# When pieces of the output weights are cast and stored, where the gate is computed, and which queue makes the first loads

## The chip, the cores and the metric

The kernel runs on one core of one Trainium2 chip. The time is the device time of one launch in microseconds (us). Three runs of the kernel before took 2896.23, 2896.97 and 2898.16 us; the median is 2896.97 us. The profiled execution took 2899.53 us, and its span from the first to the last instruction is 2897.4 us.

## The reference

One input `x` of 2048 tokens by 1024 features goes through two attention blocks of 32 heads (32 features each). A gate per token mixes their results. All in fp32.

```
qkv = x @ wqkv                          # for A and for B, each with its own weights
A: phi(t) = where(t > 0, t + 1, exp(t)) + 1e-6
   kv = phi(k)^T v ; z = sum(phi(k)) ; o = phi(q) kv / (phi(q) z + 1e-6)
   a = o @ A_wo
B: p = softmax(q k^T / sqrt(32)) ; o = p v
   b = o @ B_wo
g = sigmoid(sum(x * gate_w, -1))
out = g * a + (1 - g) * b
```

## The kernel before

**Matmuls.** A large product is made from a high and a low fp32r part of each side: three matmuls of 128x128 by 128x512 on TensorE (PE), high by high, low by high and high by low (the function `three`, L153 to L158). The split into parts is a ScalarE (ACT) cast for the high part and a subtraction on VectorE (DVE) or GpSimd (POOL) for the low part (`split`, L294 and L295).

**Stages.** (1) Until about 435 us the projections of block B, in two halves of 1024 tokens: a pass for 512 columns of v, and eight `quad`s, each a 2x2 block product by a Strassen-like scheme of seven products (X11, X21, X22, T1 to T4). The parts of x that these products read lie in pairs of the large buffers `big0` to `big13`, by the table `PLACES`. (2) From about 435 to 520 us the "v" chunk: the other columns of v, and the first row maxima of block B's scores for head 0. (3) From about 520 to 2720 us 32 heads of block B run beside the linear work of block A, which goes through the kinds "kv" (to about 1740 us), "q" (to about 2130 us) and "o". (4) At the end the output product of block B, again as a 2x2 scheme of seven products (`output`).

**A head.** For each 128x512 tile of scores PE makes it once for the row maximum (L1170; DVE reduces it out of the PSUM bank, L1175) and once for the exponential (L1312; ACT writes it to SBUF, L1315). PE then multiplies the exponentials by v (L1462, in groups of eight key tiles, some 7 us each). POOL adds up the exponentials of the key tiles (L1393, L1397), on 1536 or 512 columns at a time; DVE adds the last 512 columns in a PSUM bank (L1413), inverts the sum (L1244) and scales the result (L1247). Six or seven PSUM banks are shared by maxima, exponentials and linear work (`take`, `give`).

**What sets the order.** The kernel writes every engine's instructions in a fixed order that its own planner makes while the program is built. It keeps an assumed clock for each engine (`T`), appends work to an engine with an assumed cost (`use`), and holds back DVE work in a list `later` with a due time, cost and rank (`defer`); `fill` appends such an item when the assumed DVE clock leaves room. The chip then runs the fixed order; only semaphores decide the times. Transfers that are written with `dma` all go in order through SyncE's queue (SP, L170): a transfer that waits for its buffer holds up those behind it. `dma_start` on `nc.gpsimd` uses POOL's queue.

**Weights of the output product.** Its right sides are W11, W12, W22 and four sums S1 to S4 of blocks of `b_wo`. `wo_sums` makes the sums on POOL in the two halves of the buffer `zrep` (L501 to L523), by way of loads and stores on POOL's queue. In order of the program it stands beside the first half's quads, but POOL has nothing before it that waits for them. Later, during "o", `pre_split` takes 28 pieces (seven right sides, four pieces each) of 128x512: it loads a piece through SP, casts it on ACT (L1508) when the assumed clock is 4.5 us past the load, subtracts on DVE (L1511, deferred), and appends the two stores to SP together with the subtraction. `load_w_op` loads the finished right sides back, in the order of `w_next`.

**The gate.** `gate` loads `gate_w` to all partitions, and in the "v" chunk 16 tiles of x (128x1024) through SP into the halves of `big12`; DVE multiplies each by `gate_w` and sums along the row (L534).

**First loads of the heads.** For heads 0 and 1 the stacked parts of q and k (`load_q`, `load_k`: 36 transfers) go through SP in the "v" chunk, from the list `first`.

**Share of the linear work.** `rates` says how many linear matmuls go with each step of the heads; `RESERVE` (56.0) is the part that is held for after the heads.

Of the kernel before, what the change touches and what calls it, by code (L numbers as in the profile page):

```python
# [10 lines left out]
F32 = mybir.dt.float32  # L11
# [8 lines left out]
P = 128  # L20
# [9 lines left out]
RESERVE = 56.0  # L30
# [8 lines left out]
WARM = 8  # L39
NE = 3  # L40
# [8 lines left out]
def kernel(  # L49
# [258 lines left out]
    PLACE = [(6, 7), (8, 9), (10, 11), (12, 13), (0, 1), (2, 3), (4, 5)]  # L308
# [182 lines left out]
    def wo_piece(m, i):  # L491

        if m[0] == "S":
            return so_d[m][i]
        half, l = int(m[1]) - 1, int(m[2]) - 1
        return b_wo[(2 * i + l) * P:(2 * i + l + 1) * P, half * C:(half + 1) * C]

    def wo_sums():

        z0, z1 = halves(zrep)  # L500
        load = lambda z, m, i: nc.gpsimd.dma_start(z, wo_piece(m, i))  # L501
        for _ in range(NP):
            yield
        for i in range(KH):
            load(z0, "W21", i)
            load(z1, "W22", i)
            yield
            nc.gpsimd.tensor_add(z1, z0, z1)
            load(z0, "W11", i)
            nc.gpsimd.dma_start(so_d["S1"][i], z1)  # L510
            yield
            nc.gpsimd.tensor_sub(z1, z1, z0)
            load(z0, "W12", i)
            nc.gpsimd.dma_start(so_d["S2"][i], z1)
            yield
            nc.gpsimd.tensor_sub(z0, z0, z1)
            load(z1, "W21", i)
            nc.gpsimd.dma_start(so_d["S4"][i], z0)
            yield
            load(z0, "W11", i)  # L520
            yield
            nc.gpsimd.tensor_sub(z0, z0, z1)
            nc.gpsimd.dma_start(so_d["S3"][i], z0)  # L523
            yield

    def gate():
        xn = halves_of(big_tile(12, F32))
        junk = halves_of(big_tile(13, F32))[0]
        dma(zrep, bass.AP(tensor=gate_w.tensor, offset=gate_w.offset, ap=[[0, P], [1, D]]))
        for t in range(NT):  # L530
            dma(xn[t % 2], x[t * P:(t + 1) * P, :])
            yield
            use("dve", 1.2)
            nc.vector.scalar_tensor_tensor(junk, xn[t % 2], 1.0, zrep, op0=ALU.mult, op1=ALU.mult,  # L534
                                           accum_out=g_sb[:, t:t + 1])
        nc.scalar.activation(g_sb, g_sb, AF.Exp, scale=-1.0)
        nc.vector.tensor_scalar_add(g_sb, g_sb, 1.0)
        nc.vector.reciprocal(g_sb, g_sb)
        nc.vector.tensor_scalar(omg_sb, g_sb, -1.0, 1.0, op0=ALU.mult, op1=ALU.add)
# [123 lines left out]
    quads(0, lambda: load_pair(raw_x1[0], 1, 0), spill_rest(0), wo_sums())  # L663
# [46 lines left out]
    quads(1, lambda: load_v1(raw_a, range(KH)), spill_rest(1))  # L710
    load_v1(raw_b, range(KH, NK))

    def leave():

        split_v1(raw_a[2], 2)
        split_v1(raw_a[3], 3)
        yield
        xh_t[2] = sb.tile([P, 2 * HK * P], F32R, name="xh")
        split_v1(raw_a[0], 0)
        split_v1(raw_a[1], 1)  # L720
        yield
        for k in range(KH, NK):
            split_v1(raw_b[k - KH], k)
            yield


# [234 lines left out]
    quad(1, QUADS - 1, leave())  # L961
    T["sp"] = 0.0
    for m in range(3):
        xp_ready[m] = 0.0

    def linear():
        extra = iter(())
        gates = gate()
        first = deque()
        for h in range(2):  # L970
            first.append(lambda h=h: load_q(h, 0))
            first.append(lambda h=h: load_k(h, 0))
            first.append(lambda h=h: load_q(h, 1, NJ))
            first.extend(lambda h=h, j=j: load_k(h, j) for j in range(1, NJ))
            first.append(lambda h=h: load_v(h))
        for n, (i, t) in enumerate(units):
# [18 lines left out]
            for k in range(NK):  # L995
# [11 lines left out]
                if kind == "v":  # L1007
                    if first and (k == 1 or k == 5 and n < TPC):
                        first.popleft()()
                    if t > 1 and (k == 3 or k == 7 and t % 2):  # L1010
                        next(gates, None)
# [54 lines left out]
            elif kind == "q":  # L1066
                yield from keys_alone(n - 3)
# [53 lines left out]
    def load_q(h, j, j1=0):  # L1121

        g, r = divmod(h, 4)
        j1 = max(j + 1, j1)
        q, sl = q_cols(h, j, j1), slice(j * C, j1 * C)
        if h < (2 if j else 3):
            nc.gpsimd.memset(f32(q[3 * DH:, :]), 0.0)  # L1127
        else:
            dma(f32(q[3 * DH:3 * DH + 2, :]), f32(q[3 * DH + 2:3 * DH + 4, :]))
        for b, p in enumerate((0, 0, 1)):  # L1130
            dma(f32(q[b * DH:(b + 1) * DH, :]), qk_d[0][p][g][r * DH:(r + 1) * DH, sl])
        for i in range(j, j1):
            q_ready[h][i] = max(T["pe"] + 8.0, T["sp"] + 5.0)

    def load_k(h, j):

        g, r = divmod(h, 4)
        k = k_stack[h % 2]
        if h < 2 and j == 0:
            nc.gpsimd.memset(f32(k[3 * DH:, :]), 0.0)  # L1140
            nc.gpsimd.memset(f32(k[3 * DH:3 * DH + 2, :]), 1.0)
        sl = slice(j * C, (j + 1) * C)
        for b, p in enumerate((0, 1, 0)):
            dma(f32(k[b * DH:(b + 1) * DH, sl]), qk_d[1][p][g][r * DH:(r + 1) * DH, sl])
        k_ready[h][j] = max(T["pe"] + 6.0, T["sp"] + 4.0)
# [344 lines left out]
    coming_p, pair_at, piece_at = deque(), [0.0, 0.0], [0.0]  # L1490
    piece_t = [(mid[0], mid[1]), (mid[6], mid[9])]

    def pre_split():

        if lin_kind[0] != "o" or not (pieces or coming_p):
            return
        n = 4 * len(OPS) - len(pieces)
        if pieces and piece_at[0] <= T["pe"] and pair_at[n % 2] is not None and pair_at[n % 2] <= T["pe"] and s_done[0] > st_done[0]:
            m, i = pieces.popleft()
            dma(piece_t[n % 2][0], wo_piece(m, i))  # L1500
            coming_p.append((m, i, n % 2, T["pe"] + 4.5))
            pair_at[n % 2] = None
            piece_at[0] = T["pe"] + PIECE_STEP
        if coming_p and coming_p[0][3] <= T["pe"]:
            m, i, place, _ = coming_p.popleft()
            raw, hi = piece_t[place]
            at = use("act", 0.63, T["pe"])
            nc.scalar.copy(f32r(hi), raw)  # L1508

            def low(end):  # L1510
                nc.vector.tensor_sub(f32r(raw), raw, hi)  # L1511
                for p, src in enumerate((hi, raw)):
                    dma(wo_d[m][p][:, i * C:(i + 1) * C], src)
                pair_at[place] = end + 4.0

            defer(low, at, 0.9, 2)
# [25 lines left out]
    w_next = ["W11", "S1", "W12", "S3", "W22", "S2", "S4"]  # L1542

    def load_w_op():

        if st_done[0] < (H - 1) * NT * NJ or pieces or coming_p:
            return
# [209 lines left out]

    streams = {"lin": linear(), "max": maxima(), "head": heads_(), "out": output()}
# [43 lines left out]
    while streams or tasks:  # L1802
# [3 lines left out]
        pump_w()  # L1806
        fold_now()
# [70 lines left out]
```

## Time and profile before

| | |
|---|---|
| median of three runs | 2896.97 us |
| profiled execution | 2899.53 us |
| its span | 2897.4 us |
| PE busy | 2827.8 us, 98% |
| DVE busy | 2366.6 us, 82% |
| ACT busy | 1622.7 us, 56% |
| POOL busy | 1961.9 us, 68% |
| mean granted TensorE clock | 0.99 |

How to read the rows shown below. A row of the stretches gives the start and end of a stretch, its length, then for each of PE, PEld (weight load), DVE, ACT and POOL the busy time and the number of instructions, then the mean clock that TensorE was granted (1.00 is full speed), the busy share of the DMA engines and GB/s. In a row of the waits stand the waiting engine with what its instruction writes and its line, then who ended the wait, the total in us, how many waits, the longest. A row of the timeline has start, duration, engine, line, operation, output<-input, how many equal instructions in a row, and in brackets the idle time of the engine before it and what ended that. Groups by line end with busy us, mean ns of one | idle time before them and who ended it. "SPq" is SyncE's queue; its duration there is the time until the transfer was handed over.

### The profile page before, as it was taken

The numbers are of one execution on the slowest core, as the hardware profiler recorded it, in microseconds if no ns is written. First come the engines' busy times: TensorE is split into PE (matmuls) and PEld (weight loads), VectorE is DVE, ScalarE is ACT, GpSimd is POOL, SyncE is SP. The second block draws the span as 40 slices with busy tenths as digits, with TensorE's granted clock in tenths as the row PEclk, the third lists the DMA queues.
The fourth block names the chain that finished last, engine by engine and source line by source line (L and its number), as shares of the span: only waits on it lengthen the run. The fifth ranks groups of instructions, "written<-read, shape, count | busy, mean of one in ns | idle before, by whom it ended". The sixth has DMA issues, their size and how long they took to land.

```text
span 2897.4 us, 46873 instructions
## 1 busy us (share of the span) xinstructions
PE 2827.8 (98%) x15848; PEld 2045.3 (71%) x15848; DVE 2366.6 (82%) x3805; ACT 1622.7 (56%) x3060; POOL 1961.9 (68%) x950
## 2 busy tenths in 40 slices
PE   9999998999999999999999999999988999899999
PEld 7888887767776776677677777777755666566687
DVE  7877748888888888888888888788878888898578
ACT  4334320666676666666666666666655555566422
POOL 3200010699999999998999998899887778777000
PEclk9999999999999999999999999999999999999999
DMA  9977769434433344343433344466666565655675
GB/s 322 304 241 226 221 191 299 135 107 99 120 106 100 93 110 120 96 104 106 117 99 99 102 137 144 148 197 193 178 194 177 167 177 162 182 144 177 235 223 156
DMA packets 410411, 471.57 MB, mean 163 GB/s; under 512 B 107214, under 2 KB 235470, under 8 KB 408380
## 3 DMA queue, kind: packets, MB, share of 16 engines
q1 hardware_dynamic: 393372, 444.98, 50.0%
q0 software_dynamic: 16800, 23.60, 4.4%
q8 instruction: 126, 2.06, 0.3%
q14 instruction: 113, 0.93, 0.1%
HBM read 322.17 MB, written 131.86 MB: 157 GB/s over the span
## 4 chain that ended last, share of the span: by engine, by line
PE 86%; DVE 6%; DMA 5%; issue 1%; SPq 1%; ACT 1%; ACTq 0%; DVEq 0%
PE bank L1312 15%; PE bank L1170 15%; PE bank L1462 14%; PE bank L158 13%; PE bank L153 13%; PE bank L156 13%; DVE mx L1175 2%; DVE mid L1511 1%; SPq L170 1%; DVE big L295 1%; DMA ra<-mid 1%; DMA mid<-soS 1%; DVE bank L1244 1%; DMA big<-oA 1%; DMA v<-mid 1%
## 5 line engine op out<-in xcount | busy, mean ns | idle before, releaser
L1397 POOL TENSOR_TENSOR big<-big,big 128x512 f32<-128x512 f32 (+2 forms) x694 | 1651.0, 2383 | 156.3 <-ACT big L1315 115.0
L1175 DVE TENSOR_REDUCE mx<-bank 128x1 f32<-128x512 f32 x2048 | 1303.9, 682 | 250.3 <-PE bank L1170 246.0
L1315 ACT ACTIVATE big<-bank 128x512 f32<-128x512 f32 x2048 | 1175.1, 602 | 460.5 <-PE bank L1312 399.9
L1312 PE MATMUL bank<-big,big 128*128 128x512 f32 x1888 | 749.8, 398 | 26.8 <-ACT big L1315 12.1
L1170 PE MATMUL bank<-big,big 128*128 128x512 f32 x1888 | 745.4, 395 | 13.6 <-ACT big L1315 9.2
L153 PE MATMUL bank<-big,big 128*128 128x512 f32 x1576 | 619.5, 393 | 9.1 <-ACT big L294 4.4
L156 PE MATMUL bank<-big,big 128*128 128x512 f32 x1576 | 617.8, 392 | 2.7 <-DVE big L295 2.7
L158 PE MATMUL bank<-big,big 128*128 128x512 f32 x1572 | 616.8, 392 | 0.7 <-DMA big<-oA 0.7
L1312 PEld LDWEIGHTS bank<-big,big 128*128 128x128 f32 x1888 | 356.9, 189 | 160.6 <-issue 47.1
L1462 PE MATMUL bank<-big,mid 128*32 128x512 f32 x4096 | 455.6, 595 | 0.0
L1170 PEld LDWEIGHTS bank<-big,big 128*128 128x128 f32 x1888 | 357.2, 189 | 95.1 <-ACT big L1315 13.7
L153 PEld LDWEIGHTS bank<-big,big 128*128 128x128 f32 x1576 | 298.0, 189 | 76.5 <-ACT big L294 6.7
L156 PEld LDWEIGHTS bank<-big,big 128*128 128x128 f32 x1576 | 298.0, 189 | 65.4 <-DVE big L295 3.5
L158 PEld LDWEIGHTS bank<-big,big 128*128 128x128 f32 x1572 | 297.2, 189 | 65.7 <-DVE big L295 1.5
L1462 PEld LDWEIGHTS bank<-big,mid 128*32 128x32 f32 x4096 | 142.5, 110 | 265.9 <-issue 265.9
L1413 DVE TENSOR_TENSOR bank<-bank,big 128x512 f32<-128x512 f32 x364 | 251.2, 690 | 10.8 <-ACT big L1315 9.3
L1127 POOL MEMSET big<- 32x512 f32 (+1 forms) x4 | 3.8, 952 | 230.5 <-PE bank L158 230.5
L1393 POOL TENSOR_TENSOR big<-big,big 128x1536 f32<-128x1536 f32 (+1 forms) x31 | 121.8, 3929 | 55.2 <-ACT big L1315 51.9
L153 PE MATMUL bank<-big,xh 128*128 128x512 f32 x376 | 149.2, 397 | 8.6 <-DMA xh<-xs 7.4
L294 ACT CAST big<-mid 128x512 fp32r<-128x512 f32 (+1 forms) x157 | 92.3, 616 | 116.0 <-DVE mid L1610 66.9
L295 DVE TENSOR_TENSOR big<-mid,big 128x512 fp32r<-128x512 f32 (+1 forms) x157 | 107.0, 696 | 61.1 <-ACT big L294 58.0
L156 PE MATMUL bank<-big,xh 128*128 128x512 f32 x376 | 148.2, 394 | 0.2 <-DMA big<-wa 0.2
(150 smaller groups left out, 2173.9 us busy)
## 6 DMA issues: line engine op xcount, KB each, us to landing
big<-xs SPq DMA_DIRECT2D x288, 256.0 KB
big<-qk SPq DMA_DIRECT2D x720, 64.0 KB
xh<-xs SPq DMA_DIRECT2D x144, 256.0 KB
qk<-mid SPq DMA_DIRECT2D x128, 256.0 KB
big<-oA SPq DMA_DIRECT2D x84, 256.0 KB
xs<-big SPq DMA_DIRECT2D x64, 256.0 KB
oA<-mid SPq DMA_DIRECT2D x64, 256.0 KB
big<-big POOLq DMA_DIRECT2D x50, 256.0 KB, 5.6
```

The costliest lines, as they stand in the source:

```text
L153: yield nc.tensor.matmul(ps, sh, mh_, start=(kt == 0), stop=False)
L156: yield nc.tensor.matmul(ps, sh, ml_, start=False, stop=(late and last))
L158: yield nc.tensor.matmul(ps, sl, mh_, start=False, stop=last)
L295: eng.tensor_sub(lo, src, f32(hi))
L1170: nc.tensor.matmul(bank[b], q[:, t % TPC * P:(t % TPC + 1) * P], k[:, j * C:(j + 1) * C], start=True, stop=True)
L1175: nc.vector.tensor_reduce(m[:, t, j:j + 1], bank[b], AX.X, ALU.max)
L1312: nc.tensor.matmul(bank[b], k[:, t * P:(t + 1) * P], q_cols(h, j), start=True, stop=True)
L1315: nc.scalar.activation(pr_t[i][:, j * C:(j + 1) * C], bank[b], AF.Exp, scale=SCALE)
L1393: nc.gpsimd.tensor_add(lacc[:, :qp], pr(0)[:, :qp], pr(1)[:, :qp])
L1397: nc.gpsimd.tensor_add(lacc[:, sl], lacc[:, sl], pr(t)[:, sl])
L1413: nc.vector.tensor_add(lacc[:, qp:] if t == NT - 1 else l_b[:, :n], l_b[:, :n], src)
L1462: nc.tensor.matmul(av_b[j * DH:(j + 1) * DH, :], v[:, t, :], pr(t)[:, j * C:(j + 1) * C], start=(t == 0), stop=(t == NT - 1))
```

## The change

- `pre_split`: a piece is cast when the assumed clock is 10 us past its load (was 4.5). Its two stores are kept in a list `coming_s` and appended to SP's queue at a later turn, at the earliest 2 us after the assumed end of the subtraction; the buffer pair counts as free 6 us after that end (was 4).
- `wo_sums` is cut into 24 steps. Each begins with a 128x1 copy on ACT and one on POOL that reads it, and takes four turns of the quads' side work; it runs over both halves of the projections.
- The gate leaves the "v" chunk. `gate_step`, called once in each turn of the planner, runs it during "kv": 32 half tiles of 128x512, each loaded through SP to `mid10`, multiplied and summed by one deferred DVE instruction (assumed cost 0.9), with `gate_w` in `mid8` and `mid9`.
- The 36 first loads of q and k for heads 0 and 1 go through POOL's queue (`load_first`), in the last quad.
- `PLACE` changes which buffers some products' sides have; `RESERVE` is 24.0 (was 56.0); `w_next` loads S4 and S2 before W22.

The number of matmuls is the same. ACT has 24 small copies more, POOL 24 small copies and 36 transfers more, DVE 32 instructions of 512 columns in place of 16 of 1024 and one small sum; SP has 36 transfers of q and k less, 16 of x with 1024 columns less and 32 with 512 columns more.

On SP at the start of the "v" chunk (`in_x` is x for the gate, `qk...` the q and k parts, `v1` a result, `xs` the parts of x for the next units, which PE needs). Before:

```order
L170 DMA big12_3282<-in_x 128x1024
L170 DMA big2_208<-qk0_0_0_128 32x512 x2
L170 DMA big2_208<-qk0_1_0_136 32x512
L170 DMA big12_3282<-in_x 128x1024
L170 DMA v1_161<-mid10_234 128x512
L170 DMA big3_209<-qk1_0_0_144 32x512
L170 DMA big3_209<-qk1_1_0_152 32x512
L170 DMA big3_209<-qk1_0_0_144 32x512
L170 DMA big12_3282<-in_x 128x1024
L170 DMA xh_3102<-xs0_13_76 128x512
L170 DMA xh_3102<-xs1_13_92 128x512
```

The same place after:

```order
L171 DMA big4_210<-xs1_13_92 128x512
L171 DMA v1_161<-mid10_234 128x512
L171 DMA v1_161<-mid11_235 128x512
L171 DMA v1_161<-mid10_234 128x512
L171 DMA mid2_226<-v0_160 128x16x32
L171 DMA xh_3284<-xs0_13_76 128x512
L171 DMA xh_3284<-xs1_13_92 128x512
```

The loads for the gate and for q and k no longer stand ahead of the loads of `xs`.

On SP in the "o" stretch, around the first piece of S1 (`soS1_0` is the piece, `woS1_0` and `woS1_1` its stored parts, `oA` the input of the linear units, `wa` other stores). Before:

```order
L170 DMA mid0_224<-soS1_0_260 128x512
L170 DMA oB_127<-mid11_235 32x4x128 x4
L170 DMA wa1_0_1_167<-mid8_232 32x512 x4
L170 DMA wa0_0_1_163<-big12_3952 32x512 x2
L170 DMA woS1_0_278<-mid1_225 128x512
L170 DMA woS1_1_279<-mid0_224 128x512
L170 DMA wa0_0_1_163<-big12_3952 32x512 x2
L170 DMA xh_3102<-oA0_4_99 128x512
L170 DMA xh_3102<-oA1_4_115 128x512
```

After:

```order
L171 DMA mid0_224<-soS1_0_260 128x512
L171 DMA woW11_0_276<-mid9_233 128x512
L171 DMA woW11_1_277<-mid6_230 128x512
L171 DMA xh_3284<-oA0_4_99 128x512
L171 DMA xh_3284<-oA1_4_115 128x512
L171 DMA big1_207<-qk1_0_6_150 32x512
L171 DMA big1_207<-qk1_1_6_158 32x512
L171 DMA big1_207<-qk1_0_6_150 32x512
L171 DMA mid6_230<-soS1_1_261 128x512
L171 DMA woS1_0_278<-mid1_225 128x512
L171 DMA woS1_1_279<-mid0_224 128x512
```

The stores of a piece now stand behind the load of the next piece and behind loads for the linear units.

On DVE in "kv", around the 159th row maximum (`mx` is the maximum, `bank7` the sum of the last 512 columns). Before:

```order
L1175 TENSOR_REDUCE mx0_199<-bank6_244 128x1
L1413 TENSOR_TENSOR bank7_245<-bank7_245,big7_3941 128x512
L1175 TENSOR_REDUCE mx0_199<-bank1_239 128x1
L1175 TENSOR_REDUCE mx0_199<-bank4_242 128x1
L1175 TENSOR_REDUCE mx0_199<-bank3_241 128x1
L1175 TENSOR_REDUCE mx0_199<-bank0_238 128x1
```

After:

```order
L1193 TENSOR_REDUCE mx0_199<-bank1_239 128x1
L1193 TENSOR_REDUCE mx0_199<-bank5_243 128x1
L553 SCALAR_TENSOR_TENSOR mid10_234,g_sb_197<-mid10_234,mid8_232 128x512
L1193 TENSOR_REDUCE mx0_199<-bank3_241 128x1
L1193 TENSOR_REDUCE mx0_199<-bank4_242 128x1
L1193 TENSOR_REDUCE mx0_199<-bank0_238 128x1
```

A gate instruction with two inputs in SBUF (`mid10`, `mid8`) now stands in a run of maxima. There are 32 of these in "kv": 11 of them next to the inverse, the scaling or the other work that lies around a group of products with v, and 21 within a run of maxima.

The diff, cut to its core:

```diff
-RESERVE = 56.0
+RESERVE = 24.0
+GATE_STEP = 12.0
-    PLACE = [(6, 7), (8, 9), (10, 11), (12, 13), (0, 1), (2, 3), (4, 5)]
+    PLACE = [(6, 7), (8, 9), (10, 11), (0, 1), (2, 3), (12, 13), (4, 5)]
...
     def wo_sums():
         z0, z1 = halves(zrep)
+        tokens = count()
+        def step(*fns):
+            n = next(tokens) % (C // DH)
+            nc.scalar.copy(dn[0][:, n:n + 1], eps)
+            nc.gpsimd.tensor_copy(dn[1][:, n:n + 1], dn[0][:, n:n + 1])
+            for fn in fns:
+                fn()
+            for _ in range(4):
+                yield
...
+            yield from step(load(z0, "W21", i), load(z1, "W22", i))
+            yield from step(add(z1, z0, z1), load(z0, "W11", i), store("S1", z1, i))
...
-    def gate():
...
+    gate_w_t = [mid[8], mid[9]]
+    def gate_step():
+        n = gate_n[0]
+        if lin_kind[0] != "kv" or gate_at[0] is None or gate_at[0] > T["pe"] or n > 2 * NT:
+            return
...
+        t, i = divmod(n, 2)
+        xn, to = mid[10], (g_sb, omg_sb)[i]
+        dma(xn, x[t * P:(t + 1) * P, i * C:(i + 1) * C])
+        gate_at[0] = None
+        def part(end):
+            nc.vector.scalar_tensor_tensor(xn, xn, 1.0, gate_w_t[i], op0=ALU.mult, op1=ALU.mult,
+                                           accum_out=to[:, t:t + 1])
+            gate_at[0] = end + GATE_STEP
+        defer(part, T["pe"] + 9.0, 0.9, 2)
...
-    quads(0, lambda: load_pair(raw_x1[0], 1, 0), spill_rest(0), wo_sums())
+    quads(0, lambda: load_pair(raw_x1[0], 1, 0), spill_rest(0), sums_w)
-    quads(1, lambda: load_v1(raw_a, range(KH)), spill_rest(1))
+    quads(1, lambda: load_v1(raw_a, range(KH)), spill_rest(1), sums_w)
+    for _ in sums_w:
+        pass
...
         for k in range(KH, NK):
             split_v1(raw_b[k - KH], k)
+            if 0 < k - KH < 3:
+                load_first(k - KH - 1, 0)
             yield
+        load_first(0, 1)
+        load_first(1, 1)
+    def load_first(h, part):
+        if not part:
+            load_q(h, 0, now=nc.gpsimd)
+            load_k(h, 0, nc.gpsimd)
+        else:
+            load_q(h, 1, NJ, nc.gpsimd)
+            for j in range(1, NJ):
+                load_k(h, j, nc.gpsimd)
...
     def pre_split():
...
+        while coming_s and coming_s[0][0] <= T["pe"]:
+            _, m, i, parts = coming_s.popleft()
+            for p, src in enumerate(parts):
+                dma(wo_d[m][p][:, i * C:(i + 1) * C], src)
...
-            coming_p.append((m, i, n % 2, T["pe"] + 4.5))
+            coming_p.append((m, i, n % 2, T["pe"] + 10.0))
...
                 nc.vector.tensor_sub(f32r(raw), raw, hi)
-                for p, src in enumerate((hi, raw)):
-                    dma(wo_d[m][p][:, i * C:(i + 1) * C], src)
-                pair_at[place] = end + 4.0
+                coming_s.append((end + 2.0, m, i, (hi, raw)))
+                pair_at[place] = end + 6.0
...
-    w_next = ["W11", "S1", "W12", "S3", "W22", "S2", "S4"]
+    w_next = ["W11", "S1", "W12", "S3", "S4", "S2", "W22"]
```

100 lines of the change are left out of this document (40 added, 60 removed).

## The prediction

> **What bounds the kernel.** I read the page first, then the stretches of the span by stage, then who PE waited for in the stretches with idle time, then single waits in the timeline.
>
> ```profile
> span 2897.4 us, 46873 instructions
> PE 2827.8 (98%) x15848; PEld 2045.3 (71%) x15848; DVE 2366.6 (82%) x3805; ACT 1622.7 (56%) x3060; POOL 1961.9 (68%) x950
> ```
>
> ```profile
> 0.00:76.00 76.00, 70.46 (x291) 56.18 (x292) 54.24 (x82) 35.84 (x64) 21.84 (x31) 0.98 0.97 318
> 76.00:430.00 354.00, 354.00 (x1563) 293.10 (x1562) 249.39 (x386) 130.60 (x230) 35.60 (x39) 1.00 0.75 237
> 430.00:550.00 120.00, 109.32 (x467) 87.81 (x465) 92.88 (x157) 31.53 (x59) 16.95 (x7) 0.97 0.79 251
> 550.00:1740.00 1190.00, 1189.73 (x7661) 832.71 (x7663) 1034.61 (x1751) 793.05 (x1535) 1116.81 (x558) 1.00 0.39 106
> 1740.00:2130.00 390.00, 390.00 (x2166) 279.89 (x2159) 320.06 (x521) 247.95 (x478) 345.56 (x133) 1.00 0.56 173
> 2130.00:2660.00 530.00, 488.26 (x2637) 324.84 (x2639) 450.14 (x658) 307.31 (x554) 417.87 (x183) 0.96 0.58 166
> 2660.00:2770.00 110.00, 102.70 (x543) 69.04 (x533) 61.70 (x97) 45.72 (x89) 7.23 (x3) 0.97 0.78 265
> 2770.00:2893.00 123.00, 123.00 (x544) 101.75 (x543) 102.75 (x156) 30.71 (x54) 0.00 (x0) 1.00 0.58 177
> ```
>
> PE is the bound. The matmuls stay the same, so the time can change only by PE's idle time and by its clock. The stretches give both: idle time is length less PE busy; work lost to the clock is length times (1 - clock). That makes 5.5 + 1.5 us in the first 76 us, 10.7 + 3.6 around the "v" chunk, 0.3 in "kv", nothing in "q", 41.7 + 21.2 in "o", 7.3 + 3.3 at the change to the output product: 95 us that a change of order alone could reach. "kv" has nothing to win, only to lose.
>
> **Term 1, sums on POOL.**
>
> ```profile
> 1.33 0.73 POOL L501 DMA_DIRECT2D zrep<-in_b_wo  x1 [0.38 <-issue]
> PE bank L156 <- DVE big L295: 2.7, 1, 2.7
> PE bank L153 <- ACT mid L359: 1.7, 1, 1.7
> ACT mid L359 <- DMA v<-mid: 5.4, 3, 4.6
> L508 POOL TENSOR_TENSOR zrep<-zrep 128x512 f32<-128x512 f32 x4 | 5.3, 1314 | 23.1 <-DMA zrep<-in_b_wo 23.1
> ```
>
> POOL starts its loads at 1.33 us, beside the first loads of x and weights, with the DMA engines at 0.97. ACT then waits 5.4 us for stores of v, and PE 2.7 and 1.7 us; with the clock (1.5) that is 5.9 us. With the sums paced by the quads this traffic is gone until the first quad. I take 4.5 us of gain, between 0 and 5.9, nearer to all of it since both waits come before or with the first quad. The sums come back where PE waits for nothing (76 to 430 us, DMA 0.75, DVE 70% busy): 16 additions of 1.31 us can hold DVE up by 21 us in all, against its 105 us of idle time there, and 24 small copies on ACT stand against 223 idle us. Costed at nothing; if that cover failed, at most some 5 us.
>
> **Term 2, the "v" chunk.**
>
> ```profile
> 427.10 4.51 SPq L170 DMA_DIRECT2D big<-in_x  x1
> 435.52 1.22 DVE L534 SCALAR_TENSOR_TENSOR big<-big,zrep 128x1024 f32<-128x1024 f32 x1 [3.39 <-DMA big<-in_x]
> 436.78 0.36 SPq L170 DMA_DIRECT2D big<-in_x  x1
> 437.25 0.84 SPq L170 DMA_DIRECT2D xh<-xs  x2
> PE bank L153 <- DMA xh<-xs: 7.4, 1, 7.4
> 434.00:450.00 16.00, 8.56 (x29) 6.51 (x28) 3.80 (x7) 0.59 (x1) 0.00 (x0) 0.79 0.99 301
> ```
>
> The load of x for the gate at 436.78 could go only when DVE had done with the buffer (435.52 + 1.22), and the load that PE needs stood behind it. PE lost 7.4 us, and 16 x 0.21 = 3.4 us to the clock afterwards: 10.8. The new order of SP has no gate and no q or k loads ahead of it. I take 10; the bounds are 0 and the stretch's whole 14.3. What is late next is the same load by its own 5 to 6 us of landing, which the planner issues three units ahead. The 36 first loads cost POOL, at the 0.73 us of the row in term 1, 26 us of issue; it is 16.95 us busy from 430 to 550. They go out in the last quad, and head 0 needs the last of them only in the course of the chunk. Price 0, at most the 3 us by which the chunk's other waits could grow.
>
> **Term 3, the pieces in "o".**
>
> ```profile
> PE bank L1312 <- ACT big L1315: 12.9, 3, 8.0
> PE bank L1170 <- ACT big L1315: 9.0, 4, 5.1
> PE bank L1312 <- DVE mx L1175: 7.1, 5, 2.2
> PE bank L1312 <- DVE mid L1247: 7.0, 5, 2.3
> PE bank L1170 <- DVE mx L1175: 4.3, 3, 1.8
> ACT mid L1508 <- DMA mid<-soS: 14.9, 4, 6.0
> ACT mid L1508 <- DMA xh<-oA: 9.0, 1, 9.0
> SPq L170 <- DVE mid L1511: 35.5, 17, 4.8
> 2130.00:2150.00 20.00, 11.81 (x41) 8.53 (x40) 9.92 (x17) 7.54 (x16) 16.27 (x9) 0.74 0.58 194
> 2239.00:2251.00 12.00, 7.96 (x25) 6.01 (x24) 5.99 (x10) 4.99 (x9) 6.20 (x3) 0.72 0.80 222
> 2461.00:2473.00 12.00, 6.93 (x23) 5.14 (x22) 5.42 (x8) 4.76 (x9) 6.33 (x2) 0.72 1.04 247
> ```
>
> PE's waits have two causes. ACT stands at the cast of a piece that has not landed (L1508), the exponentials queue behind it, and PE waits for them: 12.9 + 9.0 = 21.9 us. Three of them also lower the clock: 20 x 0.26 + 12 x 0.28 + 12 x 0.28 = 12.0 us. Together 33.9. The cast now comes 5.5 us later by the assumed clock, which covers most of a single wait (6.0 and 9.0 at the longest), and SP no longer stands 35.5 us for the subtractions, so that the loads go out earlier. But the assumed clock does not know how late SP is, and the first piece still goes out behind the stores and loads at the change to "o". I take two thirds, 22, between 0 and 33.9. The DVE waits (7.1 + 7.0 + 4.3 = 18.4) stay: the subtraction itself is the same.
>
> **Term 4, the gate in "kv".**
>
> ```profile
> L1511 DVE TENSOR_TENSOR mid<-mid,mid 128x512 fp32r<-128x512 f32 x28 | 63.3, 2265 | 9.9 <-ACT mid L1508 9.9
> L295 DVE TENSOR_TENSOR mid<-mid,mid 128x512 fp32r<-128x512 f32 x64 | 44.5, 695 | 37.5 <-ACT mid L294 35.5
> 2502.90 10.95 POOL L1397 TENSOR_TENSOR big<-big,big 128x1536 f32<-128x1536 f32 x3
> 2506.55 3.97 DVE L1511 TENSOR_TENSOR mid<-mid,mid 128x512 fp32r<-128x512 f32 x1
> 2511.17 0.50 PE L1312 MATMUL bank<-big,big 128*128 128x512 f32 x1 [2.18 <-DVE mx L1175]
> DVE mx L1175 <- PE bank L1170: 139.2, 58, 5.7
> ```
>
> The same subtraction of 512 columns takes 0.695 us on average in the projections and 2.265 in "o". The timeline shows why: three POOL additions of 10.95 / 3 = 3.65 us run back to back; the second begins as the subtraction does, and the subtraction ends 0.4 us after it (2510.52 against 2510.20). It waited for POOL; the maxima behind it came late, and PE stood 2.18 us. Its inputs are both in SBUF, while the maxima and the sums of L1413 have one in PSUM. So the 18.4 us of DVE waits, and the clock that "o" lost beyond term 3 (21.2 - 12.0 = 9.2), belong to 28 subtractions: 27.6 / 28 = 0.99 us each.
>
> The gate instruction also has two inputs in SBUF. In the "v" chunk POOL was nearly idle (16.95 of 120 us); in "kv" it is busy 1116.81 of 1190 us, more than in "o" (417.87 of 530), and DVE 1034.61 of 1190. At 0.99 us each, 32 gate steps cost 32 us. Eleven of them stand beside a group of products with v, where DVE's longest idle times lie (58 waits of up to 5.7 us), and may be swallowed; POOL's higher share speaks for more at the other 21. I take 0.8 us each: 26 us of loss. The lower bound is 0: 32 x 0.7 us fit many times into the 139 us. The upper bound puts the whole wait on PE: 32 x (2.265 - 0.695) = 50 us. The 34 loads of the gate have 1190 us on SP and go far ahead of their use: 0.
>
> The Trainium skill ("SBUF — State Buffer", section "Who interferes with whom") says that a DVE instruction with two SBUF inputs contends with a GpSimd instruction that reads SBUF, and that the one that issues second is blocked until the first is done. The trace agrees for the subtraction (3.97 us against 0.695); no row shows it for the gate's multiply with a sum. By that rule the change's sum is the one below; without it the gate would be free and the sum the first rival's.
>
> **Term 5, the end.**
>
> ```profile
> PE bank L153 <- ACT big L294: 4.4, 2, 3.2
> PE bank L153 <- DMA big<-oA: 2.2, 1, 2.2
> ```
>
> The smaller reserve moves 32 matmuls of linear work ahead of the heads' end; at 354 us / 1563 matmuls (76 to 430 us) = 0.23 us each, 7.4 us. Fewer linear units then run back to back on loads of x that land late (2.2 us), but there is less to put beside the last head's sums. I take a gain of 2, between a gain of 6 and a loss of 7.4. The order of `w_next` frees no wait that a row shows: 0.
>
> **Sum.** -4.5 - 10 - 22 + 26 - 2 = -12.5 us against the profiled execution's 2899.53, so 2887.0. The median of the runs lies 2.6 below the profiled one: 2884.5, forecast 2885.
>
> **Rivals.** (a) The gate is hidden, by DVE's idle time or because its instruction does not wait for POOL: term 4 is 0, the sum -38.5, the time 2858. For it: eleven steps in places with idle time, and 139 us of DVE's idle time in the stretch. Against it: 0.99 us per subtraction in "o".
> (b) Slower: the gate's wait behind POOL lies wholly on PE, as DVE in "kv" has no slack in a run of maxima. At 1.20 us a step it eats the other 38.5 us, from 1.38 on the kernel is slower; at the full 1.57 it is 50 us, the sum +11.7, the time 2909. For it: POOL at 94%. Against it: the idle 139 us.
> (c) The pieces wait as before: the later cast meets a later load, since SP is the one that is late. Term 3 gives 8 instead of 22, the sum +1.5, the time 2898 to 2899.
>
> **How the numbers follow.** Less than 0.2% (5.8 us) cannot be told from no change here. Forecast 0.50, (a) 0.17, (b) 0.20, (c) 0.13. The forecast's own range is 2874 to 2896. The whole range reaches to both (a) and (b): 2854 to 2910. Faster (below 2891.2): 0.39 of the forecast's 0.50, (a), and 0.04 of (c): 0.60. The same: 0.10 of the forecast, 0.06 of (c): 0.16. Slower: 0.01 of the forecast, (b), 0.03 of (c): 0.24.
>
> **What would show it.** In the profile after: no wait of PE for `xh<-xs` at the start of the "v" chunk, and a clock of 1.00 there (term 2). ACT's waits at the cast of the pieces under 8 us where the two rows of term 3 add up to 23.9. The gate's instruction between 0.7 and 4 us, 2.3 on average, and PE idle 15 us or more in "kv" with waits for the maxima (term 4); a mean near 0.75 us, or idle time under 5 us there, would make the forecast wrong towards (a), idle time and lost clock over 38 us towards (b). The forecast is also wrong if PE waits in the quads, or for q and k of head 0.

## The result and the profile after

The changed kernel takes 2867.80 us (median of four runs, 2866.20 to 2869.31) against 2896.60 us for the kernel before (four runs on the same chip, 2894.55 to 2898.16). The ratio is 0.9901, 95% interval 0.9884 to 0.9918: faster, by 28.8 us. The forecast was 2885, with 2854 to 2910 as its range.

The profiled execution took 2867.15 us. The head of its page, engines with busy time, share of the span and instructions:

```profile
span 2865.4 us, 46944 instructions
PE 2814.4 (98%) x15848; PEld 2043.1 (71%) x15848; DVE 2397.1 (84%) x3838; ACT 1629.8 (57%) x3084; POOL 2007.3 (70%) x1010
```

PE is still the bound, with the same matmuls. The stretches of after, at the same borders as those of before:

```profile
0.00:76.00 76.00, 74.93 (x325) 62.47 (x326) 57.40 (x94) 40.37 (x74) 5.72 (x13) 1.00 0.88 286
76.00:430.00 354.00, 354.00 (x1563) 293.14 (x1562) 247.82 (x374) 128.72 (x245) 83.54 (x117) 1.00 0.79 251
430.00:550.00 120.00, 115.15 (x548) 88.99 (x548) 95.23 (x145) 37.98 (x72) 32.03 (x12) 1.00 0.53 170
550.00:1740.00 1190.00, 1173.61 (x7489) 822.79 (x7488) 1067.08 (x1776) 778.30 (x1508) 1102.57 (x546) 1.00 0.41 112
2130.00:2660.00 530.00, 514.04 (x2890) 346.78 (x2883) 456.12 (x696) 331.43 (x595) 442.18 (x189) 0.99 0.62 182
2660.00:2770.00 110.00, 102.29 (x490) 75.21 (x489) 71.76 (x113) 41.66 (x79) 0.00 (x0) 0.97 0.69 226
```

PE's idle time fell from 5.5 to 1.1 us in the first 76 us, from 10.7 to 4.9 around the "v" chunk and from 41.7 to 16.0 in "o"; it rose from 0.3 to 16.4 in "kv". At the change to the output product it stayed (7.3 and 7.7). The clock rose from 0.96 to 0.99 in "o" and from 0.97 to 1.00 around the "v" chunk.

Since work moves over those borders, a second measure follows the heads. DVE scales a head's result once for each head (L1247 before, L1265 after), 31 times in the trace. The rows of that instruction in before and in after, with the least, the median and the greatest duration in ns, and the first and the last start in us:

```profile
L1247 DVE TENSOR_TENSOR mid<-mid,bank x31: 686/686/689, 619.5 to 2680.8; 128x512 f32<-128x512 f32 x31
```

```profile
L1265 DVE TENSOR_TENSOR mid<-mid,bank x31: 686/686/691, 604.8 to 2655.5; 128x512 f32<-128x512 f32 x31
```

The first one starts 14.7 us earlier, the last one 25.3, and the span ends 32.0 us earlier. Four such starts cut the run into the parts of which the prediction speaks. The table gives start less start before, in us, each from one profiled execution:

| kernel | 1st (619.5) | 15th (1512.6) | 23rd (2117.0) | 31st (2680.8) | end of span (2897.4) |
|---|---|---|---|---|---|
| after | -14.7 | +11.5 | +15.2 | -25.3 | -32.0 |
| before + pieces cast and stored later | +1.0 | +1.4 | +1.4 | -37.8 | -38.1 |
| before + gate in the heads | -6.8 | +9.0 | +9.1 | +10.0 | +10.0 |
| before + paced sums | -6.6 | -6.0 | -4.5 | -8.3 | -6.9 |
| after, reserve 56 | -14.1 | +0.6 | +1.6 | -36.8 | -37.4 |
| after, gate in the "v" chunk (POOL's queue) | -6.5 | -5.4 | -0.6 | -40.2 | -47.6 |
| the same, and pieces subtracted on POOL | -8.0 | -7.0 | +0.4 | -58.8 | -65.2 |

Up to the first mark lie the sums and the "v" chunk, from there to the 15th the gate, from the 23rd to the 31st the pieces. So after gained 14.7 us, lost 26.2 by the gate in "kv" (-14.7 to +11.5), lost 3.7 in "q", gained 40.5 in "o" and 6.7 behind the last head.

Who PE waited for in "o" (2110 to 2660 us) of after; a row has the waiting instruction, who ended the wait, the total in us, the number and the longest:

```profile
PE bank L1330 <- DMA big<-ml: 6.4, 2, 5.2
PE bank L1188 <- DVE mx L1193: 5.8, 3, 2.4
PE bank L1330 <- DVE mid L1265: 2.8, 3, 1.4
```

No row of ACT is left: the 21.9 us of waits for the exponentials are gone, and the DVE waits are 8.6 us where 18.4 stood. The first row is new: it is the transfer of the low part of the row maxima (`ml`). In the same window ACT itself waited at the cast of a piece (L1530) once, and SP for the subtraction four times:

```profile
ACT mid L1530 <- DMA mid<-in_b_wo: 7.2, 1, 7.2
SPq L171 <- DVE mid L1533: 8.2, 4, 4.4
```

### The profile page after: what moved, and what is told of

Its sections match the earlier page's. It is cut to its first block, busy times and chain, and to the rows that moved or that the text cites. A ratio compares the mean times of both kernels' runs of the same rounds, so it can differ in the third digit from the quotient of the medians.

```text
span 2865.4 us, 46944 instructions
## 1 busy us (share of the span) xinstructions
PE 2814.4 (98%) x15848; PEld 2043.1 (71%) x15848; DVE 2397.1 (84%) x3838; ACT 1629.8 (57%) x3084; POOL 2007.3 (70%) x1010
## 4 chain that ended last, share of the span: by engine, by line
PE 89%; DVE 7%; DMA 2%; issue 1%; SPq 0%; ACT 0%; ACTq 0%; DVEq 0%
PE bank L1330 15%; PE bank L1188 15%; PE bank L154 14%; PE bank L157 14%; PE bank L159 14%; PE bank L1480 14%; DVE mx L1193 3%; DVE mid L553 1%; DVE mid L1533 1%; DVE bank L1262 1%; DVE bank L1431 1%; PE bank L1252 0%; PE bank L978 0%; SPq L171 0%; PE bank L867 0%
## 5 line engine op out<-in xcount | busy, mean ns | idle before, releaser
L507 POOL COPY dn<-dn 128x1 f32<-128x1 f32 x24 | 16.1, 671 | 304.3 <-ACT dn L506 304.3
```

## The experiments

All ran three rounds beside the kernel before; ratios are to the kernel before on the same chip, with 95% intervals.

| kernel | median us | before us | ratio |
|---|---|---|---|
| before + pieces | 2861.12 | 2898.59 | 0.9864 [0.9848, 0.9880] |
| before + gate in the heads | 2907.04 | 2898.59 | 1.0025 [1.0014, 1.0036] |
| before + paced sums | 2894.12 | 2898.59 | 0.9985 [0.9975, 0.9995] |
| after, gate with one input | 2844.88 | 2898.59 | 0.9811 [0.9793, 0.9828] |
| after, cast at 4.5 us | 2900.26 | 2897.39 | 1.0012 [0.9999, 1.0024] |
| after, stores at once | 2867.06 | 2897.39 | 0.9896 [0.9878, 0.9913] |
| after, gate in "v", POOL's queue | 2849.97 | 2897.39 | 0.9834 [0.9817, 0.9852] |
| after, gate in "v", SP's queue | 2847.85 | 2896.66 | 0.9840 [0.9824, 0.9857] |
| after, pieces subtracted on POOL | 2851.32 | 2896.66 | 0.9844 [0.9829, 0.9859] |
| gate in "v" and pieces on POOL | 2832.68 | 2897.39 | 0.9777 [0.9760, 0.9793] |
| after, reserve 56 | 2863.23 | 2896.66 | 0.9887 [0.9872, 0.9901] |
| gate in "v", pieces on POOL, reserve 56 | 2837.06 | 2895.88 | 0.9795 [0.9779, 0.9812] |

### One part of the change alone, on the kernel before

**The pieces.**

```diff
-            coming_p.append((m, i, n % 2, T["pe"] + 4.5))
+            coming_p.append((m, i, n % 2, T["pe"] + 10.0))
...
-                for p, src in enumerate((hi, raw)):
-                    dma(wo_d[m][p][:, i * C:(i + 1) * C], src)
-                pair_at[place] = end + 4.0
+                coming_s.append((end + 2.0, m, i, (hi, raw)))
+                pair_at[place] = end + 6.0
```

> The kernel before with one part of the change alone: the pieces cast 10 us past their load (was 4.5) and stored at a later turn. Theory 'own stage': the whole of what the stretch 2130 to 2660 won in the changed kernel (41.7 + 21.2 us of idle time and lost clock became about 16 + 5) comes from this part; the time falls by 36 to 42 us, to 2855 to 2861 us. Rival 'interplay': this part is worth the 22 us of the prediction's term 3 (2875 us), and the rest of the gain in that stretch came from the other parts.

2861.12 us, 37.5 below before: more than the whole change gives, as the theory had it, and far from the rival's 22. Its "o" stretch, PE's waits there for ACT and DVE, and the longest of the three waits that ACT still has at the cast (L1512; the other two are 0.7 and 0.6 us):

```profile
2130.00:2660.00 530.00, 510.99 (x2872) 342.14 (x2871) 469.88 (x703) 332.42 (x603) 427.01 (x186) 0.99 0.64 186
```

```profile
PE bank L1312 <- DVE mid L1247: 6.1, 4, 2.3
PE bank L1170 <- DVE mx L1175: 4.2, 2, 2.4
PE bank L1312 <- ACT big L1315: 2.5, 1, 2.5
PE bank L1312 <- DVE mx L1175: 2.1, 1, 2.1
PE bank L1170 <- DVE mid L1247: 1.5, 1, 1.5
ACT mid L1512 <- DMA xh<-oA: 3.0, 1, 3.0
```

Waits for ACT fell from 21.9 to 2.5 us, those for DVE from 18.4 to 13.9, and the clock of the stretch rose from 0.96 to 0.99. The marks show nothing before the 23rd (+1.4) and 39.2 us between the 23rd and the 31st.

**The gate.** `gate` and its calls in the "v" chunk go, `gate_step` comes; its loads use `mid8` to `mid10`.

```diff
-                    if t > 1 and (k == 3 or k == 7 and t % 2):
-                        next(gates, None)
...
+        gate_step()
```

> The kernel before with one part alone: the gate as 32 half tiles on DVE in 'kv', nothing of it in the 'v' chunk (the first loads of q and k stay on SyncE's queue). Theory: 'kv' loses 16 us of PE idle time and 5 us of clock, the 'v' chunk wins about 9; the time rises by about 12 us, to 2909. Rival: the price in 'kv' in the changed kernel was a matter of where the steps fell; then 'kv' loses under 8 us and the time is 2896 or less.

2907.04 us, 8.4 slower; the marks have -6.8 at the first head and +15.8 from there to the 15th. The "v" chunk's wait for `xh<-xs` is gone, though q's and k's first loads still stand on SP. PE's idle time in "kv" is 9.9 us (busy 1180.15 of 1190): neither the theory's 16 nor the rival's 8, and near the 8.6 of the changed kernel with the same reserve of 56 (below).

**The sums.** `wo_sums` in 24 paced steps, nothing else.

```diff
-    quads(0, lambda: load_pair(raw_x1[0], 1, 0), spill_rest(0), wo_sums())
+    quads(0, lambda: load_pair(raw_x1[0], 1, 0), spill_rest(0), sums_w)
```

> The kernel before with one part alone: the sums of the output weights paced over both halves of the projections. Theory: the 5.9 us of idle time and lost clock in the first 76 us go, nothing comes back up to 430 us: 2890 to 2891 us. Rival: those waits come from the start of the kernel in any case (under 2 us won), 2895 to 2897.

2894.12 us, 4.5 faster, between the two ranges that were expected. At the first mark it has 6.6 us; the idle time of the first 76 us fell from 5.5 to 1.2 us, but the wait for the parts of x at the "v" chunk is 8.4 us where it was 7.4.

### Why the gate costs time

```diff
-            nc.vector.scalar_tensor_tensor(xn, xn, 1.0, gate_w_t[i], op0=ALU.mult, op1=ALU.mult,
-                                           accum_out=to[:, t:t + 1])
+            nc.vector.tensor_reduce(to[:, t:t + 1], xn, AX.X, ALU.add)
```

> The changed kernel with the gate's DVE instruction replaced by a row sum of the same 128x512 tile: one SBUF input in place of two. It leaves out the multiplication by the gate's weights. Theory 'wait behind POOL': each instruction takes about 0.68 us instead of 1.97 on average, PE idle time in 'kv' falls from 16.4 to under 3 us and its clock stays full; the time falls by 18 to 21 us, to 2847 to 2850. Rival 'any instruction more in a run of maxima': PE idle time in 'kv' stays above 10 us, the time above 2858.

2844.88 us, 23 below after and 2 below the range that was expected. This kernel leaves out the product with the gate's weights, so it only measures a cause. First the gate's instruction in after, with the least, median and greatest duration, and one step of the 32 in the timeline: DVE's step, POOL's additions beside it, and PE's first matmul after its wait:

```profile
L553 DVE SCALAR_TENSOR_TENSOR mid<-mid,mid x32: 681/1589/4790, 519.0 to 1442.5; 128x512 f32<-128x512 f32 x32
```

```profile
810.34 10.63 POOL L1415 TENSOR_TENSOR big<-big,big 128x1536 f32<-128x1536 f32 x3
817.56 3.95 DVE L553 SCALAR_TENSOR_TENSOR mid<-mid,mid 128x512 f32<-128x512 f32 x1
821.45 0.68 DVE L1193 TENSOR_REDUCE mx<-bank 128x1 f32<-128x512 f32 x1
822.18 0.50 PE L1330 MATMUL bank<-big,big 128*128 128x512 f32 x1 [2.52 <-DVE mx L1193]
```

The three additions take 10.63 / 3 = 3.54 us each; the last one starts at 817.43, just ahead of the gate step, and ends at 820.97. The step ends 0.5 us later, the maximum behind it comes late, and PE stands 2.52 us. Now one of the two forms of the instruction with one input (the other took 0.662 to 0.685 us), and PE's longest wait in "kv" of that kernel:

```profile
L553 DVE TENSOR_REDUCE g_sb<-mid x16: 664/674/676, 520.2 to 1392.9; 128x1 f32<-128x512 f32 x16
```

```profile
PE bank L1187 <- DVE mx L1192: 6.1, 1, 6.1
```

In the same place of the order, with the same loads, the instruction with one SBUF input takes 0.66 to 0.69 us and never longer. PE's idle time in "kv" is still 6.7 us, where under 3 was expected, and 10.2 us at half clock go with it. Nearly all of it is one wait at the end of the gate's chain, which after has in another form (below).

The edit also takes away the 512 columns that the instruction writes to SBUF. The scaling of a head (L1265) writes as many, with one input in SBUF and one in PSUM, and took 0.686 to 0.691 us each time, although in 21 of the 31 cases an addition of POOL ran beside it. So two inputs in SBUF are what the long instructions have and the short ones do not; the product itself, with one input outside SBUF, was not tried. The rule of the Trainium skill ("SBUF — State Buffer", section "Who interferes with whom"), that a DVE instruction with two SBUF inputs contends with a GpSimd instruction that reads SBUF, and one with at most one SBUF input does not outside the modes that use two ports, agrees with 4.79 against 0.69 us at the longest.

### Which part of the pieces' edit does it

**The cast at 4.5 us again**, in the changed kernel:

```diff
-            coming_p.append((m, i, n % 2, T["pe"] + 10.0))
+            coming_p.append((m, i, n % 2, T["pe"] + 4.5))
```

> The changed kernel with the cast of a piece due 4.5 us past its load again, the stores still at a later turn. Theory 'cast': the exponentials queue behind a cast whose piece has not landed, and only the later cast takes that away; ACT's waits at the cast come back, 15 to 34 us of them, and the time rises by 15 to 30 us, to 2883 to 2898. Rival 'stores': SyncE's queue was late because it stood 35.5 us for the subtractions; with the stores later the loads are early enough; the time stays under 2875.

2900.26 us: one constant takes back 32 us, 2 more than the theory's range. The longest waits of ACT at the cast and of PE for ACT and DVE in "o", and the group of the subtraction (busy us, mean ns | idle before):

```profile
ACT mid L1530 <- DMA mid<-in_b_wo: 11.3, 4, 7.4
ACT mid L1530 <- issue: 4.2, 1, 4.2
```

```profile
PE bank L1188 <- DVE mx L1193: 6.8, 6, 1.8
PE bank L1188 <- ACT big L1333: 6.8, 4, 3.4
PE bank L1330 <- DVE mid L1265: 6.0, 5, 3.0
PE bank L1330 <- DVE mx L1193: 2.7, 2, 1.6
```

```profile
L1533 DVE TENSOR_TENSOR mid<-mid,mid 128x512 fp32r<-128x512 f32 x28 | 61.3, 2191 | 11.0 <-ACT mid L1530 11.0
```

ACT's waits at the cast (23.3 us in all, 7.2 in after) and PE's waits for ACT (9.9 us, none in after) are back. The subtraction takes 2.191 us on average, 1.586 in after, but also 1.986 in the kernel before with the pieces' edit alone. So the time of the cast also moves the subtraction against POOL's additions, and it is not alone in that; why it meets fewer of them in after was not isolated.

**The stores at once again**, in the changed kernel:

```diff
-                coming_s.append((end + 2.0, m, i, (hi, raw)))
-                pair_at[place] = end + 6.0
+                for p, src in enumerate((hi, raw)):
+                    dma(wo_d[m][p][:, i * C:(i + 1) * C], src)
+                pair_at[place] = end + 4.0
```

> The changed kernel with the two stores of a piece appended to SyncE's queue together with the subtraction again (buffer pair free 4 us later), the cast still 10 us past the load. Theory 'cast': ACT still finds its pieces landed; SyncE's queue stands for subtractions (20 to 35 us in all), but PE loses under 6 us: 2868 to 2874. Rival 'stores': loads are late again, 2880 to 2895.

2867.06 us, the same as after. SP's wait for the subtraction in "o" grew threefold and cost nothing:

```profile
SPq L171 <- DVE mid L1533: 25.6, 12, 6.0
```

### Where the gate is cheapest, and what the "v" chunk waited for

**The gate back in the "v" chunk, its loads on POOL's queue.**

```diff
+        nc.gpsimd.dma_start(zrep, bass.AP(tensor=gate_w.tensor, offset=gate_w.offset, ap=[[0, P], [1, D]]))
+        for t in range(NT):
+            nc.gpsimd.dma_start(xn[t % 2], x[t * P:(t + 1) * P, :])
+            yield
...
-        gate_step()
```

> The changed kernel with the gate back in the 'v' chunk as 16 tiles of 128x1024, where POOL computes nothing, but with its loads on POOL's queue, so that SyncE's queue does not stand for them. Theory: 'kv' wins its 16 us of idle time and 5 us of clock back, the 'v' chunk stays at 5 us of idle time: 2846 to 2850. Rival: the 16 loads of 512 KB and DVE's 1.2 us per tile bring the waits of the 'v' chunk back (10 us or more): 2857 or more.

**The same on SP's queue**, with `dma` in place of `nc.gpsimd.dma_start`:

> The changed kernel with the gate back in the "v" chunk, its loads on SP's queue as before the change; q and k of heads 0 and 1 stay on POOL's queue. Against the same with the gate's loads on POOL's queue (2850.0). If it was the gate's loads, waiting for DVE to free their buffer, that held up the load PE needed (term 2), the wait of 7 us and some 3 us of lower clock at 435 us come back: 2860 (2857 to 2863). If it was rather the sum of the many q and k loads ahead, the time stays at 2850 (2847 to 2853).

2849.97 and 2847.85 us: alike, and 18 to 20 below after. In "kv" PE is then busy 1189.87 of 1190 us in both. The first expectation was right in its time, though not in that the "v" chunk would stay as it was; the second was wrong in its time, though the wait it named did come back. The stretches 415 to 430 and 430 to 440 us of after, of the gate on SP's queue and of the gate on POOL's queue, the longest waits of PE at this place (425 to 550 us) in the last two, and in the first of these SP's waits for the gate (410 to 445 us):

```profile
415.00:430.00 15.00, 15.00 (x68) 12.43 (x67) 0.00 (x0) 1.17 (x2) 2.31 (x5) 1.00 0.79 208
430.00:440.00 10.00, 9.87 (x43) 7.83 (x43) 6.92 (x11) 1.17 (x2) 0.00 (x0) 1.00 0.73 219
```

```profile
415.00:430.00 15.00, 13.33 (x59) 10.70 (x57) 3.23 (x5) 1.57 (x3) 2.97 (x6) 1.00 0.95 259
430.00:440.00 10.00, 5.65 (x12) 3.97 (x13) 1.70 (x4) 0.00 (x0) 0.00 (x0) 0.68 0.93 266
...
PE bank L154 <- DMA xh<-xs: 5.6, 1, 5.6
PE bank L154 <- DMA big<-xs: 2.1, 1, 2.1
SPq L171 <- DMA big<-in_x: 7.8, 3, 7.1
SPq L171 <- DVE big L535: 5.8, 4, 1.8
```

```profile
415.00:430.00 15.00, 12.31 (x55) 9.87 (x53) 2.46 (x4) 1.18 (x2) 4.81 (x11) 1.00 0.91 245
430.00:440.00 10.00, 8.78 (x30) 6.50 (x30) 2.47 (x4) 0.59 (x1) 1.53 (x3) 0.83 1.01 284
...
PE bank L154 <- DMA xh<-xs: 3.2, 1, 3.2
PE bank L1173 <- DVE mx L1178: 2.4, 1, 2.4
```

With the gate's loads the DMA engines are busy 0.91 to 1.01, without them 0.73 to 0.79, whichever queue the loads go through; PE then waits for the parts of x. On SP's queue the gate's loads again hold up what stands behind them (7.8 and 5.8 us). On POOL's queue SP has no such wait, and still PE waits for the parts of x and the time is no better. So the place in the queue is not all of it; the bytes of the gate's loads (16 of 512 KB) are the likely rest, but no run has the loads without the gate's DVE work. By the first mark the gate in the "v" chunk costs 8 us (-6.5 and -6.9 against -14.7), in "kv" some 25 (+26.2 against +1.1).

### The subtraction of the pieces on POOL

**In the changed kernel:**

```diff
-            def low(end):
-                nc.vector.tensor_sub(f32r(raw), raw, hi)
-                coming_s.append((end + 2.0, m, i, (hi, raw)))
-                pair_at[place] = end + 6.0
-            defer(low, at, 0.9, 2)
+            end = use("pool", 1.33, at)
+            nc.gpsimd.tensor_sub(f32r(raw), raw, hi)
+            coming_s.append((end + 2.0, m, i, (hi, raw)))
+            pair_at[place] = end + 6.0
```

> The changed kernel with one edit: the subtraction of the 28 pieces in "o" is made by POOL instead of DVE; the gate stays in the heads. If the subtraction's waits behind POOL's additions are what "o" still loses (PE idle 16 us and some 5 us of clock there), POOL, which makes both in turn, cannot wait for itself: DVE's maxima are never late for a piece, PE is busy 523 us or more of the 530, and the time is 2867.8 - 17 = 2851 (2845 to 2856), the same step as between the two kernels with the gate in the "v" chunk (2850.0 and 2832.7). Rival: POOL's own sums come late by 28 pieces of 1.3 us or more, and part of that is paid: 2858 to 2866.

**The same edit with the gate in the "v" chunk (POOL's queue):**

> As the kernel with the gate in the 'v' chunk and its loads on POOL's queue, and the subtraction of a piece in 'o' runs on POOL in place of DVE. Theory 'wait behind POOL': on POOL it stands in order behind the additions, no maximum stands behind it; the DVE waits of PE in 'o' (8.5 us, and about 5 us of clock) go: 2834 to 2840. Rival: POOL, busy 442 of 530 us in 'o', becomes late by 28 x 1.3 us, and the buffers of the exponentials come free late: the same time as without this edit, or more.

2851.32 us, 16.5 below after, and 2832.68 us, 17.3 below the same kernel without it; the second is a little below the range that was expected. The "o" stretch of the first one and the only row of PE's waits there (2110 to 2650 us):

```profile
2130.00:2660.00 530.00, 524.55 (x3001) 356.55 (x2993) 434.63 (x694) 342.89 (x619) 470.08 (x217) 1.00 0.65 189
...
PE bank L1330 <- DMA big<-ml: 5.5, 3, 3.6
```

PE waits for DVE no longer. The kernel with both edits is the fastest here: 64.7 us below the kernel before and 35 below the changed kernel.

### The reserve

```diff
-RESERVE = 24.0
+RESERVE = 56.0
```

> The changed kernel with the reserve of linear work back at 56 (term 5 alone). The prediction's price of 2 us: 2870. By the stretches of the two traces, which are alike at the end (PE idle 7.3 and 7.7 us, clock 0.97 in both), it is worth nothing: 2866 to 2870. Were the old reserve to cost all that the bound gave, 6 us: 2874.

> The kernel with the gate in the "v" chunk (loads on POOL's queue) and the pieces' subtraction on POOL, 2832.7 us, with the reserve back at 56. In the changed kernel the old reserve gave 4.6 us, and the stretches put that into "kv" (PE idle 8.6 us instead of 16.4, one half-clock stretch instead of three), where another order of the same gate steps met POOL's additions less often. If that is the cause, the reserve has nothing to win where no gate runs in the heads: 2832.7, from 2829 to 2836. Rival: the old reserve is better by itself, at the end or in "q": 2828 or less.

In the changed kernel the old reserve is 4.6 us faster, in the fastest kernel 4.4 us slower; in each pair the intervals of the ratios overlap, so the medians alone say so. Both expectations missed. The marks and the "kv" stretch show two effects against each other. The first row is that stretch with reserve 56:

```profile
550.00:1740.00 1190.00, 1181.44 (x7533) 822.19 (x7535) 1067.60 (x1795) 784.96 (x1520) 1110.23 (x552) 1.00 0.42 112
```

The reserve of 24 gains at the end: 6.7 us behind the last head in after, 0.6 with 56. But in the order that it makes, the same 32 gate steps cost PE 16.4 us in "kv", with 56 only 8.6; the lost clock adds to that (last section), and the marks give 26.2 against 14.7. The gate's instruction takes 1.73 us on average with 56, 1.97 with 24. Without a gate in "kv" only the gain is left (6.4 us behind the last head with 24, 0.1 with 56). How the gate's steps fall against POOL's additions is thus worth some 11 us, as far as one trace of each kernel shows.

## Why the prediction was right or wrong

The direction was right, the size not: -32.0 us of span against a sum of -12.5. By the marks the 19.5 us between them split as follows.

- **Term 3, the pieces: the step that failed.** Its mechanism was right and its size was not: it took 22 of gain; the marks have 40.5 in after and 39.2 with the pieces' edit alone, whose runs gave 37.5. Two steps made it too small. The first is the third that was held back ("I take two thirds"), 11.9 us: with the pieces alone PE's waits for ACT fell from 21.9 to 2.5 us, and in after none is left. The reason given for the discount, that SP is late and so the loads too, did not hold: with the stores at once SP waits 25.6 us for the subtractions and the time is the same. The late first piece did come (7.2 us of ACT in after) without a wait of PE for ACT. The second is the sentence that the DVE waits "stay": with the pieces alone they fell by 4.5 us (18.4 to 13.9), and of the 15.9 us that the clock of "o" gave back (530 us at 0.96, then at 0.99) 3.9 are more than the 12.0 put down to ACT. In after the DVE waits fell further, to 8.6 us; with the reserve of 56 they are 14.6, so this is not the pieces' doing alone. A reading was short as well: ACT's waits at the cast before are 34.4 us, of which the two rows shown (23.9) are a part.
- **Term 1** took 4.5, the upper end was 5.9; the marks have 6.6, the runs of the part alone 4.5.
- **Term 2** took 10; with the sums' 6.6 taken off, the first mark leaves 8.1. No wait for `xh<-xs` stands there and the clock is 1.00, as foretold. Its cause was only half right: the gate's loads, but not only by their place in SP's queue, and not the q and k loads (with the gate alone moved, the first mark has 6.8 and the wait is gone). Moving the first loads to POOL's queue was rightly costed at nothing.
- **Term 4** took +26; the marks have +26.2, of which 1.1 is not the gate. The mechanism, waits behind POOL, was borne out by the kernel with one input. The end of the gate's chain, which the sum had at nothing, holds one of PE's waits (3.00 us, last section). The mean of the instruction was said to be 2.3 us and is 1.97, and PE's idle time was to be 15 us or more and is 16.4. The agreement is in part luck: in the order with the reserve of 56 the same steps cost 14.7. (In the row it rests on, the subtraction ends 0.3 us after POOL's addition, not 0.4.)
- **Term 5** took -2. "q" and the end together have -3.0 (+3.7 - 6.7). Its effect on where the gate's steps fall (some 11 us) was not seen; it lies inside term 4.
- **The rivals.** (a) comes nearest in time (2858), by luck and for a wrong reason: the gate was not hidden. (b), the whole wait on PE, is refuted by 26 against 50 us. (c), the later cast meets a later load, is refuted by ACT's wait of 7.2 us at the cast in place of 34.4.

The parts alone add up to -37.5 + 8.4 - 4.5 = -33.6 us, the whole gave -28.8; the difference of 4.8 is as large as the 4.6 that the reserve takes by way of the gate's order, but the intervals of these four ratios (0.0010 to 0.0017 to each side, 3 to 5 us) leave it within their noise.

## What to carry to other kernels

ACT, which works in order, stood at the cast of a load that had not landed, and the exponentials behind it, PE and PE's clock paid for that: one constant was worth 32 us here. An instruction on data from a transfer is thus best written for a late landing rather than for a usual one; only 4.5 and 10 us were tried. A DVE instruction with two SBUF inputs was cheaper where POOL was idle, and the subtraction on POOL itself; its price was less its duration than what stood behind it. Before a wait on a queue is costed, look whether anybody waits for the queue: 25.6 us of it cost nothing.

## What the runs showed of the hardware

**The clock after a short wait.** In after PE waited 2.52 us until 822.18. The rows give the clock behind it, and behind two other waits in "kv" (2.66 and 3.15 us):

```profile
823.00:826.40 3.40, 3.40 (x10) 2.61 (x9) 2.27 (x5) 1.73 (x4) 3.34 (x1) 0.50 0.20 61
1178.00:1181.40 3.40, 3.40 (x9) 2.51 (x9) 3.40 (x7) 2.16 (x6) 1.52 (x2) 0.50 0.45 154
1447.70:1451.10 3.40, 3.16 (x7) 2.16 (x7) 3.37 (x7) 1.16 (x2) 3.32 (x2) 0.50 0.16 40
```

Each of these waits cost a further 1.7 us (3.40 at half clock), 5.1 us for the three. The length of a wait alone does not decide: later in the same trace PE waited 3.00 us, and the clock behind it stayed at 1.00.

```profile
1465.99 0.50 PE L1188 MATMUL bank<-big,big 128*128 128x512 f32 x1 [3.00 <-DVE mx L1193]
1466.00:1476.00 10.00, 10.00 (x42) 7.67 (x43) 10.00 (x18) 7.44 (x15) 3.08 (x2) 1.00 0.22 72
```

In the clock record of this trace each of the three slow stretches lasts 3.413 us, and they start 104 and 79 times 3.413 us apart. So where a wait falls between such steps may matter; that was not tried. The Trainium skill ("TensorE: Matmul & The Clock Gate", section "Part 1: The HAM clock gate", in the table of the two states) has a half rate after an idle window of about 3.4 us; the length of the slow stretch agrees, but waits below 3.4 us were enough here.

**A small instruction behind POOL.** The end of the gate's chain in after holds an addition of 1.0 on 128x16 elements (L542). POOL's additions beside it:

```profile
1454.22 10.60 POOL L1415 TENSOR_TENSOR big<-big,big 128x1536 f32<-128x1536 f32 x3
1461.59 3.26 DVE L542 TENSOR_SCALAR g_sb<-g_sb 128x16 f32<-128x16 f32 x1 [0.28 <-ACT g_sb L541]
1464.88 0.25 DVE L543 RECIPROCAL g_sb<-g_sb 128x16 f32<-128x16 f32 x1
```

It took 3.26 us where the instruction of the same shape behind it took 0.25, although it has one tensor input. It ends at 1464.85, 0.03 us after the third of POOL's additions (1454.22 + 10.60), and the next instruction of its own kind (L544), with POOL idle, took 0.17. In the kernel with one input, two such instructions beside POOL's additions took 3.24 and 3.17 us; PE's wait of 6.1 us falls in them. That POOL held them up was not isolated by a run.
